# The last head's output weights: one half on partitions 0 to 63 alone, loaded by eight transfers of eight rows

## The chip, the cores and the metric

The kernel runs on one core of a Trainium2 chip. The metric is the device time of one execution in microseconds (us), the median over several runs. All numbers of the profile come from one further execution that the hardware profiler recorded.

## What is computed

One token (a row of 448 numbers) goes through a decode step. The reference, cut to what matters:

```python
xn = layernorm(x)
q  = (xn @ wq) -> 16 heads of 256;  k, v = k_cache, v_cache        # 8 kv heads, 65536 positions, 256 wide
p  = softmax(q . k / 16);  o = p @ v                               # two q heads share one kv head
attn = o.reshape(1, 4096) @ wo                                     # wo is 4096 x 448
moe  = xn + sigmoid(xn @ w_r) * ((silu(xn @ w_gate) * (xn @ w_up)) @ w_down)
out  = x + attn + moe                                              # 448 numbers, bf16
```

The two caches hold 2 x 268 MB, and every byte of them is read once. The output projection `wo` has 256 rows for each of the 16 q heads. This study is about the rows of the last two q heads, 14 and 15, which belong to the last kv head.

## The kernel before, in words

**Stages.** The cache is cut into 32 units (4 for each kv head) of 128 partitions x 128 positions x 256, 8 MB each, which pass through three slots of a ring in SBUF (`ring`, `slots`, line 94). While the K units of one head are transposed and multiplied, the V units of the head before are used. After the last K unit come four V units of the last head (`pe_E`, line 633). The very last V unit is loaded in pieces of 64, 32, 16, 8 and 8 positions (`LAST`, line 15), so that TensorE has little left to do when the last bytes are there.

**Order of the work.** It is written out by hand. `O` records an instruction for an engine, `W` a wait, `item` (line 242) one or several transfers with a semaphore. Every large load is issued by SyncE (SP) in the order in which `item` is called, on one queue, and each waits only for its buffer to come free. A transfer's rows are spread over 16 DMA engines; each of them works through its own share of the queue in order, and the semaphore rises by 1 as each has done its part (by 16 in all).

**The end.** In the order of SP's queue, behind the last pieces of V, stand four loads of `wo` into `kt_all`, a buffer that the K stage no longer needs:

- `wx` (line 312): the rows of kv head 6, 3584 bytes for each of 128 partitions;
- `we0` (`ENDS`, lines 313 to 315): head 14, 1792 bytes for each of 128 partitions (rows 2p and 2p+1 of the head go to partition p);
- `we1` and `we2`: head 15, its even rows and its odd rows, 896 bytes for each of 128 partitions each time.

`ps_s` holds the 448 outputs in four groups of 112 columns on four partitions, so each step of the projection is four matmuls of 112 columns, one for each group (`fin`, `part`, lines 833 to 838). At the end TensorE does this, in order:

- the last 8 positions of V directly, 16 matmuls that add to the transposed result in `ps_m` (`pv_direct`, line 607), while VectorE copies the rest of the result out of `ps_o` (`dve_ob`, line 660);
- 4 matmuls that add this copy, transposed, to the same columns of `ps_m` (`pe_oT`, line 665); VectorE scales them into `oT_sb` (line 686). Column f of head i there holds elements 2p+f of the head on partition p;
- `FIN_X` (line 900): 16 matmuls with `wx`;
- `FIN` 0, 1, 2 (line 909): 8, 4 and 4 matmuls with what `we0`, `we1` and `we2` brought, each group waiting for its load.

Then VectorE and ScalarE copy the sums to SBUF (lines 922 and 923), SP and ScalarE each send one half of the output row, and SP waits for it.

Of the kernel before, what the change touches and what calls it, by code (L numbers as in the profile page):

```python
# [4 lines left out]
BF16 = mybir.dt.bfloat16  # L5
FP32 = mybir.dt.float32
ACTF = mybir.ActivationFunctionType
ALU = mybir.AluOpType
# [4 lines left out]
CH = 64  # L13
# [8 lines left out]
def bass_parallel_sum__gqa_block_cached__moe_arch_mod__decode_kernel(  # L22
# [20 lines left out]
    P = 128  # L43
    _, Hkv, Sk, Dh = A_k_cache.shape
    D = A_x.shape[-1]
    HqDh = A_wq.shape[1]
    Hq = HqDh // Dh
    rep = Hq // Hkv
    F = B_w_gate.shape[1]
    NH = Dh // P  # L50
# [13 lines left out]
    NT = U * (Hkv - 1)  # L64
# [9 lines left out]
    OROWS = 32 * (NG - 1) + 2 * rep  # L74
# [11 lines left out]
    def S_(name, shape, dtype):  # L86
        t = nc.sbuf_tensor(name, shape, dtype)
        sb.append(t)
        return t.__enter__()
# [4 lines left out]
    slots = [ring[:, i * SLOT:(i + 1) * SLOT] for i in range(NSLOT)]  # L94
# [6 lines left out]
    wo_end = kt_all[:, 0:WON]  # L101
    temp = [WQN]

    def T_(n, dtype=BF16):
        n2 = n if dtype == BF16 else 2 * n
        a = slots[2][0:1, temp[0]:temp[0] + n2]
        temp[0] += n2
        assert temp[0] <= SLOT - P
        return a if dtype == BF16 else a.bitcast(dtype)
# [3 lines left out]
    p_sb = S_("p_sb", [P, HC, CH, rep], BF16)  # L113
# [2 lines left out]
    ones_f = S_("ones_f", [P, P], FP32)  # L116
    sel_bf = S_("sel_bf", [P, NG, rep], BF16)
    sel2_bf = S_("sel2_bf", [P, 2, rep], BF16)
    zero_bf = S_("zero_bf", [P, 2 * rep], BF16)
    x_row = T_(D)  # L120
    wr_row = T_(D)
    xe_row = T_(2 * NE * P).rearrange("o (t r p) -> o t r p", t=2, r=NE)
# [22 lines left out]
    hT_sb = S_("hT_sb", [P, 2 * FH], BF16)  # L145
    ob_sb = S_("ob_sb", [P, 2 * Dh], BF16)
    oT_sb = S_("oT_sb", [P, NH, rep], BF16)
    x_f, xc_f, xn_f = T_(D, FP32), T_(D, FP32), T_(D, FP32)
    xn_bf = T_(D)
    stat = S_("stat", [1, 16], FP32)  # L150
# [20 lines left out]
    ps_m = PS_("ps_m", [P, 512], FP32)  # L171
    C_XNT, C_BC, C_TOT, C_OT, C_Q, C_BIG = 0, 16, 18, 22, 28, 64
    C_HT = C_Q
    assert C_Q + NH * Hq + 4 <= C_BIG and C_HT + FK <= C_BIG and C_BIG + P <= 512

    sems = {}
# [33 lines left out]
    def W(e, *key):  # L210
        put(e, "w", key, None, None)
# [3 lines left out]
    def O(e, key, fn, sem=None, n=1):  # L215
        key = key if isinstance(key, tuple) else (key,)
        if not ghost[0]:
            weight[key] = n
        put(e, "o", key, fn, sem or e)
# [22 lines left out]
    def item(key, parts, need=()):  # L242
        for n in need:
            W("sp", *n)
        for ap, src, sem in parts:
            semtot[sem] = semtot.get(sem, 0) + 16
            items[key] = (sem, semtot[sem])
            prog["sp"].append(("d", here[0], ("DMA", key, len(prog["sp"])), (ap, src), sem))
# [16 lines left out]
    def flat_src(src, n):  # L265
        return src.rearrange("a b -> (a b)").rearrange("(p n) -> p n", p=P)

    def wo_src():
        return A_wo[(Hq - rep) * Dh:Hq * Dh, :].rearrange("(i p f) n -> p i f n", i=rep, f=NH)

    def wo_view(t):
        return t.rearrange("p (i f n) -> p i f n", i=rep, f=NH)

    def wo_rows(h0, h1):

# [34 lines left out]
        slot_item("v", t, 0, list(zip(LAST_SEMS, LAST)) if t == NU - 1 else [("slot0", CH), ("half0", CH)],  # L310
                  {c: [("PVC", t - 1, c)] for c in range(HC)})
    item("wx", [(wo_x, wo_rows(HL, HL + 1)[:, 0, :, :].rearrange("p f n -> p (f n)"), "wx")], [("HT",)])
    ENDS = [(0, 0, NH), (1, 0, 1), (1, 1, NH)]
    for k, (i, f0, f1) in enumerate(ENDS):
        item(("wo_end", k), [(wo_view(wo_end)[:, i, f0:f1, :], wo_src()[:, i, f0:f1, :], "we%d" % k)])
    for g, e in enumerate(("sp", "act")):
        late.append((e, g))
    items["out"] = ("out", 16 * len(late))
# [1 line left out]
    def W_item(e, key):  # L320
        W(e, "DMA", key)
# [102 lines left out]
    def mm(*a, **k):  # L424
        return pe.matmul(*a, **k)  # L425
# [181 lines left out]
    def pv_direct(slot, c, lo, hi):  # L607
        def f(it):
            kv = slots[slot].rearrange("p (j d) -> p j d", d=Dh)
            for j in range(lo, hi):  # L610
                for hf in range(NH):
                    ins = mm(ps_m[0:P, C_OT + hf * rep:C_OT + (hf + 1) * rep],
                             lhsT=kv[:, j, :].rearrange("p (d f) -> p d f", f=NH)[:, :, hf], rhs=p_sb[:, c, j - c * CH, :],
                             start=False, stop=False, skip_group_check=True)
            return ins
        return f

# [47 lines left out]
    def pe_oT(t):  # L665
        W("pe", "OB", t)
        W("pe", "RS", min(t, NT))

        def f(it):
            for hf in range(NH):  # L670
                c = C_OT + hf * rep
                for n2 in range(2):
                    lhsT = ob_sb[0:OROWS, n2 * Dh:(n2 + 1) * Dh].rearrange("r (p f) -> r p f", f=NH)[:, :, hf]
                    ins = mm(ps_m[0:P, c:c + rep], lhsT=lhsT, rhs=sel2_bf[0:OROWS, n2, :],
                             start=(n2 == 0 and t < NT), stop=(n2 == 1), skip_group_check=(t >= NT))
            return ins

        O("pe", ("OT", t), f)
        W("dve", "OT", t)
        W("dve", "RS", min(t, NT))  # L680
        src = ps_m[0:P, C_OT:C_OT + NH * rep].rearrange("p (f i) -> p f i", f=NH)
        if t < NT:
            O("dve", ("OTSB", t), lambda it: nc.vector.tensor_tensor(
                out=oT_all[:, :, bass.ds(it[0] * U + it[1], 1), :].rearrange("p f o i -> p f (o i)"), in0=src, in1=rs[:, :, :], op=ALU.mult))
        else:
            O("dve", ("OTSB", t), lambda it: nc.vector.tensor_tensor(out=oT_sb[:, :, :], in0=src, in1=rs[:, :, :], op=ALU.mult))

    def pick(nj):
        return s2[0][:, 0:nj * P] if nj > rep else s2[1][:, 2 * P:2 * P + nj * P]
# [143 lines left out]
    def part(rows, k, g):  # L833
        o = k * D + COLS[g] * DQ
        return rows[:, o:o + DQ]

    def fin(g):
        return ps_s[32 * g:32 * g + 1, 0:DQ]
# [30 lines left out]
    def sums(T):  # L869
        pe_attn2()  # L870
        W_item("dve", "wd")
        O("dve", "XN_AGAIN", lambda it: nc.vector.tensor_scalar(out=xn_again, in0=x_again, scalar1=stat[0:1, 7:8], scalar2=stat[0:1, 4:5],
                                                                op0=ALU.add, op1=ALU.mult))
        W("dve", "XN_AGAIN")
        W("dve", "FFN2")
        W("dve", "ATTN")
        W("dve", "SIG")
        O("dve", "YS", lambda it: nc.vector.scalar_tensor_tensor(  # L878
            out=sum_f, in0=ps_y, scalar=stat[0:1, 6:7], in1=xn_again, op0=ALU.mult, op1=ALU.add))
        W("dve", "YS")  # L880
        O("dve", "YX", lambda it: nc.vector.tensor_tensor(out=sum_f, in0=sum_f, in1=x_again, op=ALU.add))
        W("dve", "YX")
        O("dve", "SUM", lambda it: nc.vector.tensor_tensor(out=sum_f, in0=ps_a, in1=sum_f, op=ALU.add))
        W("pe", "SUM")
        W("pe", "SCOPY", T)

        def fin_base(it):
            for g in range(NF):
                ins = mm(fin(g), lhsT=ones_f[0:1, 0:1], rhs=part(sum_f, 0, g), start=True, stop=False,
                         tile_position=(0, 32 * g), skip_group_check=True)  # L890
            return ins

        O("pe", "FIN_BASE", fin_base)
        O("pe", "OT_ZERO", lambda it: mm(ps_m[0:P, C_OT:C_OT + NH * rep], lhsT=s2[0][:, 0:P], rhs=zero_bf[:, 0:NH * rep], start=True, stop=True,
                                         skip_group_check=True))

    def finish(T):
        W_item("pe", "wx")

        def fin_x(it):  # L900
            for f in range(FO):
                for g in range(NF):
                    ins = mm(fin(g), lhsT=oT_h[:, HL * FO + f:HL * FO + f + 1], rhs=part(wo_x, f, g), start=False, stop=False,
                             tile_position=(0, 32 * g), skip_group_check=True)
            return ins

        O("pe", "FIN_X", fin_x)
        W("pe", "OTSB", T)
        for k, (i, f0, f1) in enumerate(ENDS):
            W_item("pe", ("wo_end", k))  # L910

            def f(it, k=k, i=i, f0=f0, f1=f1):
                for hf in range(f0, f1):
                    for g in range(NF):
                        ins = mm(fin(g), lhsT=oT_sb[:, hf, i:i + 1], rhs=part(wo_end, i * NH + hf, g), start=False,
                                 stop=(k == len(ENDS) - 1), tile_position=(0, 32 * g), skip_group_check=True)
                return ins

            O("pe", ("FIN", k), f)
        W("dve", "FIN", len(ENDS) - 1)  # L920
        W("act", "FIN", len(ENDS) - 1)
        O("dve", "RESULT", lambda it: nc.vector.tensor_copy(out=res_bf[:, DQ:2 * DQ], in_=ps_s[64:97, 0:DQ]), "res")
        O("act", "RESULT2", lambda it: nc.scalar.activation(out=res_bf[:, 0:DQ], in_=ps_s[0:33, 0:DQ], func=ACTF.Copy), "res")
        alias("dve", "RES", sem="res")
        for e, g in late:
            W(e, "RES")
            prog[e].append(("d", here[0], ("OUT", g), (out[0][:, 2 * g * DQ:2 * (g + 1) * DQ], res_bf[32 * g:32 * g + 1, :]), "out"))
# [296 lines left out]
```

## Time and profile before

| | |
|---|---|
| time before, median of 3 runs | 1275.82 us (1275.75 to 1275.88) |
| the profiled execution's own time | 1275.79 us |
| its span, from the first to the last instruction | 1274.5 us |
| busy: TensorE matmul (PE) | 952.0 us (75%) |
| busy: VectorE (DVE), ScalarE (ACT) | 575.6 us (45%), 436.8 us (34%) |
| busy: SP's DMA queue (q1) | 99.8% of 16 engines' span |
| moved | 549.16 MB, mean 431 GB/s |
| granted TensorE clock, mean | 0.894 |

The views of the profile name each operation by its line in the kernel, its engine, its tiles (out<-in) and its shape; nearly all matmuls stand under line 425, the helper that records them, so they are told apart by tiles. PEld is TensorE's loading of weights, which runs beside its matmuls. A view over a stretch of time gives for DMA the share of 16 engines that were busy and the GB/s that they moved.

### The profile page before, as it was taken

What the parts mean: (1) busy time and instruction counts of PE and PEld (TensorE: products, weight loads), DVE (VectorE), ACT (ScalarE), POOL (GpSimd) and SP (SyncE); (2) the same over time, 40 slices, a digit from 0 to 9 for tenths busy, and PEclk for the clock granted to TensorE, in tenths of its full rate; (3) what the DMA queues carried; (4) which work ended last, traced back from release to release, by engine and by line L of the source; (5) the groups of instructions that cost most, each with busy time, mean ns of one, the idle gap of its engine ahead of it and who ended that gap; (6) DMA issues with size and microseconds to landing.
All of it is one profiled execution on the core that took longest, in us unless ns stands there. A gap on an engine that the chain in (4) does not pass through costs nothing.

```text
span 1274.5 us, 23415 instructions
## 1 busy us (share of the span) xinstructions
PE 952.0 (75%) x9665; PEld 620.3 (49%) x9665; DVE 575.6 (45%) x1088; ACT 436.8 (34%) x656; POOL 8.1 (1%) x38
## 2 busy tenths in 40 slices
PE   4998977778777679777778776787777687777754
PEld 2676654445544455444455444454444454444421
DVE  5665644345444455343454444453444544434410
ACT  2454533244332434223333243343333334323300
POOL 2000000000000000000000000000000000000000
PEclk9999998899888899888898888898888998878876
DMA  9999999999999999999999999999999999999998
GB/s 408 428 433 440 436 430 430 436 428 444 432 432 428 436 428 446 432 430 430 434 432 442 432 430 432 432 438 438 430 430 432 432 442 434 430 430 436 418 431 373
DMA packets 12643, 549.16 MB, mean 431 GB/s; under 512 B 1367, under 2 KB 1754, under 8 KB 2906
## 3 DMA queue, kind: packets, MB, share of 16 engines
q1 hardware_dynamic: 12628, 549.03, 99.8%
q8 instruction: 6, 0.10, 0.0%
q14 instruction: 3, 0.02, 0.0%
q10 hardware_dynamic: 6, 0.00, 0.0%
HBM read 549.03 MB, written 0.00 MB: 431 GB/s over the span
## 4 chain that ended last, share of the span: by engine, by line
DMA 77%; PE 19%; ACT 2%; issue 1%; DVE 1%; SPq 0%; ACTq 0%; DVEq 0%
DMA ring<-in_A_v_cache_dram 71%; PE ps_o L425 13%; DMA ring<-in_A_k_cache_dram 5%; PE ps_t L425 3%; PE ps_q L425 2%; ACT kt_all L489 2%; DMA kt_all<-in_A_wo_dram 1%; PE ps_m L425 1%; DVE kt_all L487 0%; ACT S_sb L570 0%; SPq L973 0%; PE ps_s L425 0%; DVE m1p L540 0%; DVE S_sb L538 0%; DVE ring L878 0%
## 5 line engine op out<-in xcount | busy, mean ns | idle before, releaser
L425 PE MATMUL ps_t<-ident_f,ring 128*128 128x128 f32 x4096 | 585.7, 285 | 83.0 <-DMA ring<-in_A_k_cache_dram 59.6
L487 DVE COPY kt_all<-ps_t 128x1024 bf16<-128x1024 bf16 x768 | 487.0, 685 | 290.9 <-PE ps_q L425 286.7
L425 PEld LDWEIGHTS ps_t<-ident_f,ring 128*128 128x128 f32 x4096 | 449.6, 143 | 234.9 <-issue 135.3
L489 ACT ACTIVATE kt_all<-ps_t 128x1024 bf16<-128x1024 bf16 x256 | 262.2, 1024 | 501.0 <-PE ps_q L425 501.0
L425 PE MATMUL ps_o<-ring,p_sb 128*4 128x512 bf16 x2044 | 178.8, 511 | 211.2 <-DMA ring<-in_A_v_cache_dram 206.8
L425 PEld LDWEIGHTS ps_o<-ring,p_sb 128*4 128x4 bf16 x2044 | 53.4, 102 | 301.2 <-issue 277.1
L425 PE MATMUL ps_q<-kt_all,q_cur 128*2 128x512 bf16 x2056 | 164.1, 396 | 0.4 <-DVE kt_all L487 0.3
L511 ACT ACTIVATE s<-ps_q 98x512 bf16<-98x512 f32 x257 | 151.8, 591 | 1.3 <-PE ps_q L425 1.3
L593 DVE RECIPROCAL rs<-ps_m 128x4 f32<-128x4 f32 x29 | 5.3, 183 | 273.8 <-PE ps_m L425 273.8
L580 ACT ACTIVATE p_sb<-S_sb 128x128 bf16<-128x128 bf16 x64 | 18.9, 307 | 273.2 <-PE ps_o L425 273.0
L425 PEld LDWEIGHTS ps_s<-sel_bf,s 128*128 128x128 bf16 x1032 | 64.1, 97 | 5.1 <-ACT s L511 1.9
L425 PE MATMUL ps_s<-sel_bf,s 128*128 128x8 bf16 x1032 | 63.3, 167 | 1.3 <-ACT s L511 1.3
L663 DVE CAST ob_sb<-ps_o 100x512 bf16<-100x512 f32 x29 | 20.1, 692 | 88.8 <-PE ps_o L425 88.8
L425 PEld LDWEIGHTS ps_q<-kt_all,q_cur 128*2 128x2 bf16 x2056 | 26.4, 79 | 45.0 <-issue 45.0
L425 PEld LDWEIGHTS ps_m<-rowsum,ones_f 128*128 128x128 f32 x58 | 12.1, 261 | 21.3 <-issue 21.3
L489 ACT ACT_TABLE_LOAD x7 | 9.0, 1283 | 26.0 <-PE ps_q L425 26.0
L540 DVE TENSOR_REDUCE m1p<-S_sb (+1 forms) x33 | 13.9, 422 | 4.4
L425 PE MATMUL ps_m<-rowsum,ones_f 128*128 128x4 f32 x58 | 14.6, 323 | 0.0
L538 DVE CAST S_sb<-ps_s 128x256 f32 (+1 forms) x33 | 13.7, 415 | 1.9 <-PE ps_s L425 1.9
L570 ACT ACTIVATE S_sb<-S_sb,negmax 128x512 bf16<-128x512 bf16 x16 | 13.2, 852 | 3.2 <-DVE negmax L564 3.2
L425 PE MATMUL ps_m<-diag,ones_f 2*128 2x2 f32 x58 | 11.2, 260 | 3.8 <-DVE diag L555 0.8
L425 PEld LDWEIGHTS ps_m<-diag,ones_f 2*128 2x128 f32 x58 | 8.7, 187 | 10.6 <-DVE diag L555 10.6
(98 smaller groups left out, 126.9 us busy)
## 6 DMA issues: line engine op xcount, KB each, us to landing
ring<-in_A_k_cache_dram SPq DMA_DIRECT2D x10, 4096.0 KB, 28.6
ring<-in_A_v_cache_dram SPq DMA_DIRECT2D x5, 4096.0 KB, 15.7
ring<-in_A_wq_dram SPq DMA_DIRECT2D x1, 2688.0 KB, 11.1
ring<-in_A_wo_dram SPq DMA_DIRECT2D x1, 2688.0 KB, 29.0
ring<-in_A_v_cache_dram SPq DMA_DIRECT2D x1, 2048.0 KB, 10.8
ring<-in_B_w_gate_dram SPq DMA_DIRECT2D x1, 1568.0 KB, 16.7
ring<-in_B_w_up_dram SPq DMA_DIRECT2D x1, 1568.0 KB, 20.0
ring<-in_B_w_down_dram SPq DMA_DIRECT2D x1, 1568.0 KB
```

The lines of the kernel that those rows point to most:

```text
L425: return pe.matmul(*a, **k)
L487: O(e, ("EV", s, m), lambda it: nc.vector.tensor_copy(out=kt[:, :], in_=tb[:, :]), f"ev{m}")
L489: O(e, ("EV", s, m), lambda it: nc.scalar.activation(out=kt[:, :], in_=tb[:, :], func=ACTF.Copy), f"ev{m}")
L511: O("act", ("EVQ", s), lambda it: nc.scalar.activation(out=s2[s % 2][0:QROWS, :], in_=ps_q[0:QROWS, :], func=ACTF.Copy), "evq")
L538: O("dve", ("SCOPY", u), lambda it: nc.vector.tensor_copy(out=S_sb[:, at(it, SBN), :], in_=ps_sn), "sc")
L540: O("dve", ("SMAX", u), lambda it: nc.vector.tensor_reduce(out=m1p[:, :, at(it, 1)], in_=S_sb[:, at(it, SBN), :].rearrange("p n i -> p i n ...
L570: O("act", ("EXP", h, i), lambda it, i=i: nc.scalar.activation(out=S_sb[:, :, i], in_=S_sb[:, :, i], func=ACTF.Exp, bias=negmax[:, i:i + 1 ...
L580: O("act", ("PC", t, c), lambda it: nc.scalar.activation(out=p_sb[:, c, :, :], in_=S_sb[:, n:n + CH, :], func=ACTF.Copy), "pc")
L593: O("dve", ("RS", t), lambda it: nc.vector.reciprocal(out=rs[:, :, :], in_=ps_m[0:P, C_TOT:C_TOT + NH * rep]))
L663: O("dve", ("OB", t), lambda it: nc.vector.tensor_copy(out=ob_sb[0:OROWS, :], in_=ps_o[0:OROWS, :]))
```

## The change

Head 14 keeps its layout and its one transfer. Head 15 is cut in another way: not into even and odd rows, but into rows 0 to 127 (the low half) and rows 128 to 255 (the high half).

- The low half goes to partitions 0 to 63 only, rows 2p and 2p+1 on partition p, 1792 bytes for each. It is loaded by eight transfers that share one semaphore (`we0`); transfer j brings partitions j, j+8, ... j+56. They now stand first, behind `wx`.
- Head 14's transfer comes second (`we1`).
- The high half comes last (`we2`): one row of 896 bytes on each of 128 partitions, into a part of the ring that is free by then (`wo_high`).

For the high half the result is needed in another layout (element 128+p on partition p), for head 15 alone. It goes into one more column of `ps_m` (`C_OTX`), with 8 more matmuls in `pv_direct`, 2 more in `pe_oT`, and one more VectorE operation that scales it into `oT_x`. `FIN` 0 is now 8 matmuls with 64 partitions, `FIN` 1 is 8 with head 14, `FIN` 2 is 4 with the high half and waits for `oT_x` too. The diff without declarations:

```diff
-    ENDS = [(0, 0, NH), (1, 0, 1), (1, 1, NH)]
-    for k, (i, f0, f1) in enumerate(ENDS):
-        item(("wo_end", k), [(wo_view(wo_end)[:, i, f0:f1, :], wo_src()[:, i, f0:f1, :], "we%d" % k)])
+    PL = P // NH
+    low = wo_src(Hq - 1)[0:P, :].rearrange("(p f) n -> p (f n)", f=NH)
+    ENDS = [[(wo_end[j:PL:8, NH * D:2 * NH * D], low[j:PL:8, :]) for j in range(8)],
+            [(wo_end[:, 0:NH * D], wo_src(Hq - 2).rearrange("(p f) n -> p (f n)", f=NH))],
+            [(wo_high, wo_src(Hq - 1)[P:2 * P, :])]]
+    for k, parts in enumerate(ENDS):
+        item(("wo_end", k), [(to, src, "we%d" % k) for to, src in parts])
...
+                ins = mm(ps_m[0:P, C_OTX:C_OTX + 1], lhsT=kv[:, j, P:2 * P], rhs=p_sb[:, c, j - c * CH, rep - 1:rep],
+                         start=False, stop=False, skip_group_check=True)
...
+            for n2 in range(2 if t >= NT else 0):
+                ins = mm(ps_m[0:P, C_OTX:C_OTX + 1], lhsT=ob_sb[0:OROWS, n2 * Dh + P:n2 * Dh + 2 * P],
+                         rhs=sel2_bf[0:OROWS, n2, rep - 1:rep], start=False, stop=(n2 == 1), skip_group_check=True)
...
+            O("dve", ("OTX", t), lambda it: nc.vector.tensor_tensor(
+                out=oT_x[:, 0:1], in0=ps_m[0:P, C_OTX:C_OTX + 1], in1=rs[:, 0, rep - 1:rep], op=ALU.mult))
...
-        for k, (i, f0, f1) in enumerate(ENDS):
+        cols = [[(oT_sb[0:PL, hf, 1:2], wo_end[0:PL, :], NH + hf) for hf in range(NH)],
+                [(oT_sb[:, hf, 0:1], wo_end, hf) for hf in range(NH)],
+                [(oT_x[:, 0:1], wo_high, 0)]]
+        for k in range(len(ENDS)):
             W_item("pe", ("wo_end", k))
+            if k == len(ENDS) - 1:
+                W("pe", "OTX", T)
```

The matmul that clears these columns (`OT_ZERO`, line 894) writes 5 columns instead of 4.

More of the change, by code (lines that the diff above doesn't have):

```diff
@@ L118, in bass_parallel_sum__gqa_block_cached__moe_arch_mod__decode_kernel @@
     sel2_bf = S_("sel2_bf", [P, 2, rep], BF16)
-    zero_bf = S_("zero_bf", [P, 2 * rep], BF16)
+    zero_bf = S_("zero_bf", [P, 3 * rep], BF16)
     x_row = T_(D)
@@ L147, in bass_parallel_sum__gqa_block_cached__moe_arch_mod__decode_kernel @@
     oT_sb = S_("oT_sb", [P, NH, rep], BF16)
+    oT_x = S_("oT_x", [P, 2], BF16)
+    wo_high = slots[1][:, 0:D]
     x_f, xc_f, xn_f = T_(D, FP32), T_(D, FP32), T_(D, FP32)
@@ L173, in bass_parallel_sum__gqa_block_cached__moe_arch_mod__decode_kernel @@
     C_HT = C_Q
+    C_OTX = C_OT + NH * rep
+    assert C_OTX < C_Q and Dh == 2 * P
     assert C_Q + NH * Hq + 4 <= C_BIG and C_HT + FK <= C_BIG and C_BIG + P <= 512
@@ L266, in flat_src, with wo_src @@
         return src.rearrange("a b -> (a b)").rearrange("(p n) -> p n", p=P)
[L268 to L272, printed above, removed]
+    def wo_src(h):
+        return A_wo[h * Dh:(h + 1) * Dh, :]
     def wo_rows(h0, h1):
@@ L893, in sums @@
         O("pe", "FIN_BASE", fin_base)
-        O("pe", "OT_ZERO", lambda it: mm(ps_m[0:P, C_OT:C_OT + NH * rep], lhsT=s2[0][:, 0:P], rhs=zero_bf[:, 0:NH * rep], start=True, stop=True,
+        O("pe", "OT_ZERO", lambda it: mm(ps_m[0:P, C_OT:C_OTX + 1], lhsT=s2[0][:, 0:P], rhs=zero_bf[:, 0:NH * rep + 1], start=True, stop=True,
                                          skip_group_check=True))
@@ L908, in finish, with f @@
         W("pe", "OTSB", T)
-        for k, (i, f0, f1) in enumerate(ENDS):
+        cols = [[(oT_sb[0:PL, hf, 1:2], wo_end[0:PL, :], NH + hf) for hf in range(NH)],
+                [(oT_sb[:, hf, 0:1], wo_end, hf) for hf in range(NH)],
+                [(oT_x[:, 0:1], wo_high, 0)]]
+        for k in range(len(ENDS)):
             W_item("pe", ("wo_end", k))
-            def f(it, k=k, i=i, f0=f0, f1=f1):
-                for hf in range(f0, f1):
+            if k == len(ENDS) - 1:
+                W("pe", "OTX", T)
+            def f(it, k=k):
+                for w, rows, x in cols[k]:
                     for g in range(NF):
-                        ins = mm(fin(g), lhsT=oT_sb[:, hf, i:i + 1], rhs=part(wo_end, i * NH + hf, g), start=False,
+                        ins = mm(fin(g), lhsT=w, rhs=part(rows, x, g), start=False,
                                  stop=(k == len(ENDS) - 1), tile_position=(0, 32 * g), skip_group_check=True)
```

## The prediction

> **What bounds the kernel now.** The page comes first: it says which resource is full.
>
> ```profile
> span 1274.5 us, 23415 instructions
> ...
> q1 hardware_dynamic: 12628, 549.03, 99.8%
> q8 instruction: 6, 0.10, 0.0%
> ```
>
> SP's queue keeps the 16 DMA engines busy for 99.8% of the span, and the change moves the same bytes. So nothing before the last transfers can get shorter; what can move is the way in which the last bytes arrive and what follows them. The chain that ended last, from 1268 us on, shows that end:
>
> ```profile
> 1256.16 15.19 DMA kt_all<-in_A_wo_dram
> 1271.35 0.04 issue
> 1271.40 0.54 PE ps_s L425 x15
> 1271.94 0.13 issue
> 1272.07 0.78 PE ps_s L425 x14
> 1272.85 0.02 issue
> 1272.87 0.28 DVE kt_all L922
> ```
>
> The output weights land at 1271.35 and later, TensorE multiplies, VectorE copies. The timeline of the same microseconds, once as a whole and twice for shorter stretches, shows what each group of matmuls waits for (the bracket is the idle time before it):
>
> ```profile
> 1270.73 0.18 PEld L425 LDWEIGHTS ps_m<-sel_bf,ob_sb 100*128 100x128 bf16 x4
> ...
> 1271.04 0.16 DVE L686 TENSOR_TENSOR oT_sb<-ps_m,rs 128x4 bf16<-128x4 f32 x1 [0.47 <-PE ps_m L425]
> ...
> 1271.40 0.28 PEld L425 LDWEIGHTS ps_s<-kt_all,oT_h 128*1 128x1 bf16 x16 [0.48 <-DMA kt_all<-in_A_wo_dram]
> ...
> 1273.18 0.26 SPq L973 DMA_DIRECT2D out_dram<-kt_all  x1
> ```
> ```profile
> 1272.04 0.13 PEld L425 LDWEIGHTS ps_s<-kt_all,oT_sb 128*1 128x1 bf16 x8 [0.36 <-issue]
> ```
> ```profile
> 1272.29 0.09 PEld L425 LDWEIGHTS ps_s<-kt_all,oT_sb 128*1 128x1 bf16 x4
> 1272.56 0.09 PEld L425 LDWEIGHTS ps_s<-kt_all,oT_sb 128*1 128x1 bf16 x4 [0.17 <-DMA kt_all<-in_A_wo_dram]
> ```
>
> `FIN_X` starts at 1271.40, `FIN` 0 at 1272.04, `FIN` 1 at 1272.29, `FIN` 2 at 1272.56. Sixteen weight loads of `FIN_X` take 0.28 us, so TensorE alone would begin `FIN` 0 at about 1271.7; each group stands where its load landed. From 1272.56 on the rest is fixed: 0.3 us until the copy at 1272.87, and 1.6 us from there to the end at 1274.5. **The end follows the last landing, one to one.**
>
> When do the 16 engines come to the end of the queue? A view by stages of the same execution (its last two columns are the share of the 16 engines and GB/s; a share a little over 1 means that packets overlap):
>
> ```profile
> 1269.00:1269.60 0.60, 0.37 (x4) 0.09 (x4) 0.00 (x0) 0.00 (x0) 0.00 (x0) 0.50 1.01 395
> 1270.10:1270.30 0.20, 0.00 (x0) 0.00 (x0) 0.20 (x1) 0.00 (x0) 0.00 (x0) 0.50 0.93 345
> 1271.00:1271.20 0.20, 0.00 (x1) 0.00 (x0) 0.16 (x1) 0.00 (x0) 0.00 (x0) 0.50 0.55 206
> 1271.30:1271.70 0.40, 0.30 (x16) 0.28 (x16) 0.00 (x0) 0.00 (x0) 0.00 (x0) 0.50 0.41 141
> 1272.10:1272.50 0.40, 0.40 (x12) 0.16 (x12) 0.00 (x0) 0.00 (x0) 0.00 (x0) 0.50 0.00 0
> ```
>
> At 1269 all 16 engines work, 395/16 = 24.7 GB/s each. At 1271.1 it is 206 GB/s, which is eight engines; at 1271.5 it is 141, which is six; by 1272.1 none. So the engines finish over some 2 us, about eight of them before 1271 and eight after. The work was cut into equal shares, so some engines run behind. Views of the DMA at three places tell since when (each transfer ends with one packet of under 512 B on each of its engines):
>
> ```profile
> DMA packets 32, 0.52 MB, mean 477 GB/s; under 512 B 16, under 2 KB 16, under 8 KB 16
> ```
> ```profile
> DMA packets 28, 0.52 MB, mean 477 GB/s; under 512 B 12, under 2 KB 12, under 8 KB 12
> ```
> ```profile
> q8 instruction: 4, 0.07, 0.9%
> ```
>
> The first is from 20.5 to 21.6 us: all 16 engines end one transfer within 1.1 us. The second is from 59.3 to 60.4 us: only 12 do, four lag. The third is from 24 to 52 us, between them: four instruction packets of 16 KB went through the engines, and two more do from 1202 to 1213 us, as the page's six leave and this row says:
>
> ```profile
> q8 instruction: 2, 0.03, 1.2%
> ```
>
> Six instruction packets and six engines that finish last: code loading puts one engine behind each time, and a queue that never runs dry never lets it catch up.
>
> **The change part by part.** What counts is which engines carry the eight small transfers. One row tells how a transfer of few rows is spread, from 1202.7 to 1204.8 us, where 128 rows of `w_down` end and the single row of x follows them on the queue:
>
> ```profile
> DMA packets 146, 0.88 MB, mean 417 GB/s; under 512 B 17, under 2 KB 18, under 8 KB 146
> ```
>
> 17 closing packets: 16 for `w_down`, one for the single row. A one-row transfer runs on one engine, so I take it that eight rows run on eight engines, one row each, and always on the same eight, those that serve partitions 0 to 63 in a full transfer (the *lower* engines). Then a lower engine carries 8 x 1792 B more and 8 x 896 B less than before, an upper one only the 8 x 896 B less.
>
> - *The last landing, if the last engines are upper ones.* Their order becomes `wx`, head 14, high half: the old `we1` load is gone. Eight rows of 896 B cost the last engine 1272.56 - 1272.29 = 0.27 us, the distance of `FIN` 1 and `FIN` 2 (by the rate: 7168 B / 24.7 GB/s = 0.29). **-0.27 us.** The lower engines, +0.3 us, stay behind them, if they belong to those that finished by 1271.
> - *`FIN` 2 waits for two semaphores* instead of one. The only group before that does so is `FIN` 0, for which the gap is 0.13 us of issue, against 0.04 at `FIN_X`: between 0 and 0.09; I take 0.03, since the added wait is over long before. **+0.03 us.**
> - *More matmuls in front of `FIN_X`.* 8 in `pv_direct` and 2 in `pe_oT` at 0.18/4 = 0.045 us are 0.45 at most; in `FIN` 0 and 1 4 more at 0.13/8 = 0.016. What hides them: the 0.48 us in which PEld idles before `FIN_X`. Without that cover `FIN_X` would start up to 0.45 later, at 1271.85, and its 16 loads and those of `FIN` 0 and 1 (0.28 + 0.26) end at 1272.39, so that `FIN` 2 would lose 0.1 of its gain. **0.**
> - *VectorE's added operation* is one more of 0.16 us behind `oT_sb`, done some 0.6 us later than that was (two operations and the later matmuls), near 1271.8, before `FIN` 2 asks for it. **0.**
> - *SP issues 11 transfers where it issued 4.* SP's row:
>
> ```profile
> 1256.16 1.85 SPq L973 DMA_DIRECT2D kt_all<-in_A_wo_dram  x4
> ```
>
>   0.46 us each, so 7 more end at 1261.2 instead of 1258.0. A transfer with few rows may cost less (0.26 for one half of the output, above). The engines come to this place of the queue some 15.19 us after 1256.16, and the earliest of them 2 us before that. Only the output is queued on SP behind, at 1273.18. **0.**
>
> Sum: -0.24 us against this execution, 1275.79 us, which lies 0.03 below the median of the runs: **1275.55 us**.
>
> **The rivals.**
>
> *Last engines among the lower ones (slower).* If one of the six late engines serves partitions 0 to 63, the change adds to the longest queue: eight rows of 1792 B more, which took 1272.04 - 1271.40 = 0.64 us from `FIN_X` to `FIN` 0 (with the 0.13 of issue in it; by the rate 0.58), less the 0.27. That is +0.29 to +0.37 and seven more closing packets: +0.35, **1276.1 us**. It decides as soon as one lower engine lies within 0.6 us of the last. For it: six engines placed by chance would hardly all be upper ones. Against it: the engines come in two groups, eight before and eight after 1271, as two halves of the partitions would; and the one engine that can be named is an early one. From 1202.7 to 1202.8 us, the first 0.1 us of the stretch above:
>
> ```profile
> DMA packets 11, 0.05 MB, mean 520 GB/s; under 512 B 2, under 2 KB 3, under 8 KB 11
> ```
>
> The only packet between 512 B and 2 KB is the row of x, for partition 0, here with the first closing packet of the 17: its engine is the first of all. [...]
>
> *The eight transfers don't pick engines.* If an eight-row transfer is spread over all 16 or over changing engines, each carries the same bytes as before: the last landing stays where it was, within 0.05 us, **1275.8 us**. Against it stands the one closing packet of the one-row transfer. [...]
>
> *Code loads fall elsewhere.* The program grows by some 14 matmuls, 7 transfers and one VectorE operation at its end. If that makes one more 16 KB packet necessary and it meets a late engine, this engine falls back by 16 KB / 24.7 GB/s = 0.66 to 1.7 us (the lag that the late group has), less 0.27: **1276.2 to 1277.2 us**. [...] Against it: the loops, where most of the time goes, keep their code, and ten of 16 engines aren't late.
>
> **How the numbers follow.** Last engines are upper ones: 50%, 1275.4 to 1275.7. A late lower engine: 33%, 1275.9 to 1276.25. No choice of engines, or a gain eaten by the matmuls in front: 12%, 1275.7 to 1275.9. Code loads or something not seen: 5%. The predicted time is the first case's, 1275.55. The range, 1275.35 to 1276.3, takes in the first three cases and the 0.07 us by which runs differ from their median. The bound of 0.2% is 2.55 us, about what a measurement of this kernel can tell from no change; none of the first three cases reaches it, so: faster 1%, same 96%, slower 3%.
>
> **What would show it.** In the stages above the share at 1271.0 to 1271.2 should be about as high as now, the lower engines having taken over what the upper ones lost, and that at 1271.3 to 1271.7 lower. `FIN` 2 should start near 1272.3, `FIN_X` still at 1271.4. If `FIN` 2 starts at 1272.9, late engines are lower ones; if it stays at 1272.56, the transfers don't steer. If `FIN_X` itself moves by more than 0.1 us, either the matmuls in front lost their cover or the engines' lags have changed, by code loads. A change before 1268 us would refute the claim that the rest is untouched.

## The result, and the profile after

The changed kernel takes 1277.53 us (median of 22 runs, 1277.10 to 1278.84) where the kernel before takes 1275.80 (22 runs, 1275.61 to 1276.32): +1.73 us, a ratio of 1.0014 with an interval of 1.0008 to 1.0021. That is slower, by less than the 0.2% of the bound, and outside the stated range of 1275.35 to 1276.3.

The page of the profile after, its span and queue lines:

```profile
span 1276.5 us, 23452 instructions
...
q1 hardware_dynamic: 12612, 549.03, 99.6%
q8 instruction: 6, 0.10, 0.0%
```

The same bytes, and 2.0 us more span. This execution is the longest of the 22 (1278.84 us); their median span is 1276.0, where that of the kernel before is 1274.6 (33 executions timed beside the first four runs below). So the spans differ by 1.4 us by the medians, and some 0.3 of the +1.73 lie outside the span; more on that behind the experiments. The page counts six instruction packets within the span, as before. The stages of the prediction, in the changed kernel (share of 16 engines and GB/s at the end), with one stage more:

```profile
1269.00:1269.60 0.60, 0.34 (x8) 0.08 (x4) 0.00 (x0) 0.00 (x0) 0.00 (x0) 0.50 1.07 390
1270.10:1270.30 0.20, 0.02 (x4) 0.00 (x0) 0.13 (x1) 0.00 (x0) 0.00 (x0) 0.50 0.95 247
1271.00:1271.20 0.20, 0.00 (x0) 0.00 (x0) 0.00 (x0) 0.00 (x0) 0.00 (x0) 0.50 0.53 179
1271.30:1271.70 0.40, 0.40 (x15) 0.40 (x16) 0.00 (x0) 0.00 (x0) 0.00 (x0) 0.50 0.57 190
1272.10:1272.50 0.40, 0.28 (x14) 0.20 (x15) 0.21 (x2) 0.00 (x0) 0.00 (x0) 0.50 0.21 70
1272.60:1273.20 0.60, 0.30 (x16) 0.04 (x4) 0.00 (x0) 0.00 (x0) 0.00 (x0) 0.50 0.07 24
```

Until about 1269.5 all is as before. At 1270.2 the engines are just as busy as before (0.95 against 0.93) but move 247 GB/s, not 345: the packets take longer. The DMA records have them one by one: the packets of `wx` (3584 B) that start from 1269.5 to 1271.0 took 0.141 us each before (median of 54) and take 0.204 now (median of 43). What is lost there is made up late, and in the last stage one engine still works (24 GB/s), where before there was none after 1272.1. The timeline of the end:

```profile
1271.29 0.71 PEld L430 LDWEIGHTS ps_m<-p_sb,ring 128*128 128x128 bf16 x24 [1.68 <-DMA ring<-in_A_v_cache_dram]
...
1272.36 0.28 PEld L430 LDWEIGHTS ps_s<-kt_all,oT_h 128*1 128x1 bf16 x16 [0.20 <-DMA kt_all<-in_A_wo_dram]
...
1274.08 0.13 PEld L430 LDWEIGHTS ps_s<-kt_all,oT_sb 64*1 64x1 bf16 x8 [1.44 <-issue]
...
1274.39 0.10 PEld L430 LDWEIGHTS ps_s<-kt_all,oT_sb 128*1 128x1 bf16 x8 [0.18 <-DMA kt_all<-in_A_wo_dram]
1274.45 0.14 PEld L430 LDWEIGHTS ps_s<-ring,oT_x 128*1 128x1 bf16 x4
```

Two things are new. The last pieces of V and `wx`, which the change doesn't touch, land 1.0 us later: the matmuls of `pv_direct` start at 1271.29, `FIN_X` at 1272.36 instead of 1271.40. In the kernel before, `pv_direct` stood here:

```profile
1270.30 0.51 PEld L425 LDWEIGHTS ps_m<-p_sb,ring 128*128 128x128 bf16 x16 [0.98 <-DMA ring<-in_A_v_cache_dram]
```

And from `FIN_X` to `FIN` 0, the group of the eight small transfers, it is 1.72 us, not 0.64. `FIN` 1 and 2 follow closely. So the end again hangs on the landings, but it is now those of the small transfers that hold it: the last of them is at 1273.98.

### The profile page after: what moved, and what is told of

It reads as the page before. It is cut to its first block, busy times and chain, and to the rows that moved or that the text cites. A ratio compares the mean times of both kernels' runs of the same rounds, so it can differ in the third digit from the quotient of the medians.

```text
span 1276.5 us, 23452 instructions
## 1 busy us (share of the span) xinstructions
PE 955.2 (75%) x9679; PEld 620.3 (49%) x9679; DVE 577.8 (45%) x1089; ACT 436.4 (34%) x656; POOL 11.6 (1%) x38
## 4 chain that ended last, share of the span: by engine, by line
DMA 76%; PE 19%; ACT 2%; issue 1%; DVE 1%; SPq 1%; ACTq 0%; DVEq 0%
DMA ring<-in_A_v_cache_dram 71%; PE ps_o L430 13%; DMA ring<-in_A_k_cache_dram 4%; PE ps_t L430 3%; ACT kt_all L494 2%; PE ps_q L430 2%; PE ps_m L430 1%; DMA kt_all<-in_A_wo_dram 1%; SPq L990 1%; DVE kt_all L492 0%; ACT S_sb L575 0%; PE ps_s L430 0%; DVE m1p L545 0%; DVE S_sb L543 0%; DVE ring L890 0%
## 5 line engine op out<-in xcount | busy, mean ns | idle before, releaser
L430 PE MATMUL ps_o<-ring,p_sb 128*4 128x512 bf16 x2044 | 184.5, 524 | 211.3 <-DMA ring<-in_A_v_cache_dram 206.9
```

## The experiments

Each run was timed beside the kernel before on the same chip; the column on the right is the difference of the two medians. Three theories stood at the start. **P** (partitions): an engine that writes partitions which another engine writes in full transfers gets in its way. **C** (closings): each transfer closes with one packet on each of its engines, and closings of one engine land 0.2 us apart (in the changed kernel the last six from 1273.38 to 1274.38), while its data run ahead. **L**: a late engine is among the lower ones, and nothing else.

| run | engines steered to | rows on foreign partitions (by the assumption in e1) | closings per engine and group | time, us | difference, us |
|---|---|---|---|---|---|
| the change | lower eight | yes | 8 | 1277.53 | +1.73 |
| e1_own | lower eight | no | 8 | 1277.04 | +1.15 |
| e2_one64 | none | yes | 1 | 1276.62 | +0.73 |
| e3_onerow | lower eight | yes | 1 | 1277.04 | +1.15 |
| e4_block | lower eight | yes | 8 | 1277.58 | +1.69 |
| e5_labels (one execution) | none | - | - | 1277.06 | +1.08 |
| e6_onerow_own | lower eight | no | 1 | 1276.13 | +0.15 |
| e7_four | lower eight | no | 4 | 1276.15 | +0.17 |
| e8_halves | none | yes | 2 | 1276.72 | +0.74 |
| e9_eight_small | lower eight, few bytes | no | 8 | 1277.38 | +1.46 |
| e10_one_small | lower eight, few bytes | no | 1 | 1276.13 | +0.21 |
| e11_four_rows | engines 0 to 3 | no | 2 on engines 0 to 3, else 1 | 1276.06 | +0.14 |
| e12_full | none | no | 1 | 1275.98 | +0.08 |

The medians carry the comparison; the intervals of the ratios are about 0.0009 (1.1 us) to each side, so few rows are settled by their intervals alone. What settles it is that rows with one property group together, that the eleven times of e9 (1276.56 to 1277.49) and of e10 (1275.86 to 1276.43) do not overlap, and that the traces show where.

**e1_own: other rows in each transfer.**

```diff
-    ENDS = [[(wo_end[j:PL:8, ...], low[j:PL:8, :]) for j in range(8)],
+    own = [(j // 4 * 32 + j % 4, j // 4 * 32 + 32) for j in range(8)]
+    ENDS = [[(wo_end[a:b:4, ...], low[a:b:4, :]) for a, b in own],
```

> The changed kernel, with other rows in each of the eight transfers: transfer j brings partitions j, j+4, ... j+28 for j below 4, and the same of partitions 32 to 63 for the others. Rows, bytes, packets and completions of every engine stay the same; only which engine writes which partition changes. Theory P (partitions): in the changed kernel an engine writes partitions that another engine writes in all full transfers, and two engines meet at one place of SBUF; now each of the eight engines writes what it always writes, so the slow 1.5 us (229 to 246 GB/s from 1269.5 to 1271.0 at a full share) go away: about 1276.0 us, 1275.5 to 1276.3. Theory C (completions): eight transfers close eight times on each of eight engines, at 0.2 us each (the last landings of the changed kernel are 0.2 us apart): no change, 1277.3 to 1277.7 us. Theory L (a late lower engine and nothing else) gives 1277.5 as well, since the engines' loads are the same.

Measured 1277.04: neither theory's number alone. The trace splits it. Three of its stages, the first of them the time of the slow stretch in the changed kernel:

```profile
1269.50:1271.00 1.50, 1.03 (x29) 0.69 (x26) 0.69 (x1) 0.00 (x0) 0.00 (x0) 0.50 0.91 341
```
```profile
1272.00:1272.40 0.40, 0.00 (x0) 0.00 (x0) 0.00 (x0) 0.00 (x0) 0.00 (x0) 0.50 0.05 18
1272.50:1273.10 0.60, 0.00 (x0) 0.00 (x0) 0.00 (x0) 0.00 (x0) 0.00 (x0) 0.50 0.00 0
```

341 GB/s where the changed kernel has the first of these rows, and the kernel before the second:

```profile
1269.50:1271.00 1.50, 0.60 (x4) 0.09 (x4) 0.69 (x1) 0.00 (x0) 0.00 (x0) 0.50 0.95 238
```
```profile
1269.50:1271.00 1.50, 1.02 (x24) 0.61 (x20) 0.69 (x1) 0.00 (x0) 0.00 (x0) 0.50 0.81 301
```

The kernel before moves fewer GB/s than e1 only because fewer engines still have work (a share of 0.81). What compares is GB/s divided by the share: 375 in e1, 372 before, 251 in the changed kernel. So the slow stretch is gone, as P says, with nothing changed but which engine carries which rows, and so which partitions it writes (e6 against e3 below has the same source rows on every engine). If row i of each transfer goes to the same engine, this edit gives each of the eight engines four neighbouring partitions of 0 to 31 and four of 32 to 63, where the change gave it eight neighbouring ones. That the former are those which the engine writes in a full transfer was my assumption: the DMA records name no partition, and what stands for it is that the slow stretch is gone here and in e6 and e7 (333 and 334 GB/s at 0.86 and 0.87). And no packet moves after 1272.5, yet `FIN` 0 waits until 1273.15:

```profile
1271.42 0.28 PEld L431 LDWEIGHTS ps_s<-kt_all,oT_h 128*1 128x1 bf16 x16 [0.23 <-DMA kt_all<-in_A_wo_dram]
...
1273.15 0.13 PEld L431 LDWEIGHTS ps_s<-kt_all,oT_sb 64*1 64x1 bf16 x8 [1.46 <-issue]
```

In the record of the semaphore the last four increments of `we0` came at 1272.45, 1272.65, 1272.85 and 1273.05, then that of `we1` at 1273.25 and of `we2` at 1273.44: six closings of one engine, 0.2 us apart, after its data had gone through. That is theory C. The last packet of data starts at 1272.35. `wx` landed last at 1271.37, and ten closings of 0.2 us behind it end at 1273.4, so this engine is taken to be one that got `wx` last: a late engine is among the lower eight.

**e2_one64: one transfer of 64 rows.** `ENDS = [[(wo_end[0:PL, ...], low)], ...`

> The changed kernel with one transfer of 64 rows in place of the eight: the same layout and the same matmuls, but all 16 engines carry four rows each and close once. Theory C: the cost was the 64 closings, so it goes: 1275.7 to 1276.0 us. Theory P: 16 engines write to partitions 0 to 63, half of them to partitions that are not theirs, so part of the slow stretch stays: 1276.2 to 1277 us. Theory L: no engine carries more than in the kernel before: 1275.7 to 1275.9 us.

Measured 1276.62, as P has it. Its slow stretch:

```profile
1269.50:1271.00 1.50, 0.69 (x13) 0.26 (x10) 0.69 (x1) 0.00 (x0) 0.00 (x0) 0.50 1.02 262
```

**e3_onerow: one transfer of eight long rows on foreign partitions.** `ENDS = [[(slots[1][0:PL:8, D:D + 8 * NH * D], low8)], ...`

> The changed kernel with the eight transfers replaced by one of eight rows of 14336 B, to partitions 0, 8, ... 56 of the free part of the ring: each of the eight engines carries the same bytes as in the changed kernel, but in one packet, closed once. The computation is changed: FIN 0 multiplies what its buffer held before, not the low half of head 15. Theory C: one closing instead of eight, the 0.2 us steps go: 1275.6 to 1276.2 us, by whether a late engine is a lower one. Theory P: the partitions are still those of other engines, so the slow stretch stays: 1277 us or more. Theory L: 1277.5 us, the same bytes on the same engines.

Measured 1277.04, with 247 GB/s in the slow stretch: P's number, not C's. With one closing only, C cannot be the whole cause.

**e4_block: eight neighbouring partitions in each transfer.** `wo_end[8 * j:8 * j + 8, ...]`

> The changed kernel with eight neighbouring partitions in each of the eight transfers: transfer j brings partitions 8j to 8j+7. Rows, bytes and closings of every engine stay the same, but eight engines now write into eight neighbouring partitions at a time. Theory P: four engines at each place instead of two, worse than the changed kernel: 1278 us or more. Theory C and theory L: no change, 1277.3 to 1277.7 us.

Measured 1277.58, no worse than the change, with 298 GB/s in the stretch: P's number missed, that of C and L held. That more engines at one place cost more is not borne out; the engines run up to 2 us apart (the 16 landings of one transfer lie 1.94 us apart near 1258 in the trace before), so the eight rows of one transfer need not meet, but this was not tried further.

**e5_labels: which engines are late.** The kernel before with `item("mk", [(..., n rows of 20 + n elements) for n in 1..15])` behind the first loads of `wo`.

> The kernel before with 15 tiny transfers behind the first loads of wo, of 1, 2, ... 15 rows with 42 to 70 bytes each, each row length used by one transfer only: if a transfer of n rows runs on the n lowest engines, the number of such packets that an engine carries tells which engine it is. Theory L, in its sharpened form after the first four runs: of the six engines that finish last one carries rows of the lower half, five of the upper half; a lower one among them is what the steered rows must not meet. If all six were upper ones, a late lower engine could not explain the last 1.0 us of the changed kernel. Time as before, within 0.5 us.

The transfer with n rows left exactly n packets in the DMA records, and each step of n brought one engine more. Their lag behind engine 0 near 1210 us, in us:

```
engine   0    1    2    3    4    5    6    7    8    9    10   11   12   13    14
lag     0.00 0.90 0.17 0.99 0.73 1.68 1.50 0.15 0.33 2.33 1.63 1.64 0.02 -0.04 0.14
```

Late are 5, 6, 9, 10 and 11; the record can't name engine 15, and the sixth instruction packet starts at 1210.87, in the midst of this place. Two lower engines are late, so my first case, all late engines upper, does not hold in this execution. The time, 1277.06 in one execution, missed the half microsecond that I gave it: in this execution the engines' landings of one transfer lay 2.5 us apart already near 60 us (1.9 in the kernel before), and `wx` landed 0.6 to 1.6 us later on them. What the 15 small transfers did to that was not followed up.

**e6_onerow_own: the steering alone.** As e3, but `slots[1][0:32:4, ...]`, partitions 0, 4, ... 28.

> The changed kernel with the eight transfers replaced by one of eight rows of 14336 B to partitions 0, 4, ... 28, those that the eight engines write in full transfers too: the same bytes on the same engines, one closing each, no foreign partition. The computation is changed: FIN 0 multiplies what its buffer held before, not the low half of head 15. Theories P and C together: both costs are gone, only the steering is left: with one late lower engine 1276.1 us (1275.9 to 1276.3), as my prediction's first rival had it; without one 1275.55. If neither P nor C holds and the layout with 64 partitions and more matmuls costs by itself: 1276.6 us as with one transfer of 64 rows, or more.

Measured 1276.13, +0.15, against e3 with the same packets and +1.15: only the partitions differ. The slow stretch is gone:

```profile
1269.50:1271.00 1.50, 1.04 (x23) 0.53 (x24) 0.69 (x1) 0.00 (x0) 0.00 (x0) 0.50 0.86 333
```

**e7_four: four closings.** Four transfers of eight rows of 3584 B, `slots[1][j:32:4, ...]`.

> The same with four transfers of eight rows of 3584 B, partitions j, j+4, ... j+28 for transfer j: the same bytes on the same engines, four closings each, no foreign partition. The computation is changed as in the run with one transfer of eight rows. Theory C: a closing takes 0.2 us, so four take 0.8 us, about 0.2 more than the bytes (0.58): 0.2 us above the run with one closing, 0.7 below the one with eight (1277.04): 1276.3 us. If the time of a packet and not the closing counts: the same time as with one closing.

Measured 1276.15, as with one closing. Theory C in the form that I wrote down (0.2 us above e6) is not seen. That the closings do take their 0.2 us is in the trace: the last four of `we0` land at 1271.63, 1271.85, 1272.06 and 1272.27, with 0.14 us of data for each. Those of `we1` and `we2` follow at 1272.55 and 1272.83, the last 1.39 us behind the landing of `wx`, where the data of the three loads take 1.45 by the rate (0.58, 0.58, 0.29). So C has to be put otherwise: a backlog of closings costs only what the bytes behind it don't cover. Four closings take 0.8 us beside 0.58 us of data, and the two loads behind them bring 0.9 us of data with only two closings. This account was made after the result.

**e8_halves: foreign partitions in the kernel before.** Head 14's load in two transfers of 64 rows: `halves = ((0, P // 2), (P // 2, P))` for the first of `ENDS`.

> The kernel before with head 14's load cut into two transfers of 64 rows each, partitions 0 to 63 and 64 to 127: the same layout, the same matmuls, the same bytes on every engine, two closings instead of one. Theory P by itself: 64 rows on 16 engines give an engine partitions that another one writes in full transfers, so a stretch with full share and few GB/s appears, as with one transfer of 64 rows: 1276.4 to 1277 us. Theory C: one closing more, hidden behind the bytes: 1275.9 us. If the source rows or the other buffer made the slow stretch: 1275.9 us too.

Measured 1276.72, +0.74. Nothing but the cut of one transfer was changed, and the slow stretch is there:

```profile
1269.50:1271.00 1.50, 0.68 (x7) 0.17 (x7) 0.69 (x1) 0.00 (x0) 0.00 (x0) 0.50 1.01 273
```

**e9_eight_small and e10_one_small: closings in the kernel before.** `item("mk", ...)` behind `we0`: eight transfers of eight rows of 512 B, or one of eight rows of 4096 B, on the engines' own partitions by the assumption in e1.

> The kernel before with eight transfers of eight rows of 512 B added between head 14's load and the even rows of head 15; they go to a free part of the ring, on the partitions that their engines write in full transfers too, and nothing uses them. The bytes are few (4 KB on each lower engine, 0.17 us at 24.7 GB/s), the matmuls are those of before. Theory C: on a late lower engine eight closings of 0.2 us stand in front of the last two loads, 1.6 us of which the bytes of the queue cover only a part; from the landing of wx at least 11 closings, 2.2 us, where before it was 1.16: about 1.0 us more, 1276.7 to 1277.1 us. If closings are free and the extra of the changed kernel's eight transfers lay in their rows or in the new layout: 1276.0 to 1276.2 us.

> The same with one transfer of eight rows of 4096 B at the same place: the same bytes on the same engines, one closing instead of eight. Both theories: 1276.0 to 1276.2 us, by the 0.17 us of bytes on a late lower engine. Theory C is the difference to the run with eight small transfers, 0.6 us or more; without it the two runs agree.

Measured 1277.38 and 1276.13: the same bytes, 1.25 us apart. The first lies above the 1277.1 that theory C gave. Three of its eleven executions took only 1276.6, which was not followed up. The group behind the small transfers, `FIN` 1, in the run with eight (where `FIN` 2 follows in the same row) and in the run with one:

```profile
1273.87 0.29 PEld L428 LDWEIGHTS ps_s<-kt_all,oT_sb 128*1 128x1 bf16 x8 [1.62 <-DMA kt_all<-in_A_wo_dram]
```
```profile
1272.66 0.09 PEld L427 LDWEIGHTS ps_s<-kt_all,oT_sb 128*1 128x1 bf16 x4 [0.28 <-DMA kt_all<-in_A_wo_dram]
```

In the run with eight, the last packet of data starts at 1272.31, and the increments go on until 1274.03. At the end two engines step side by side, 0.2 us each (1273.39 and 1273.43, 1273.59 and 1273.63), so the distance belongs to the engine and not to the semaphore. Head 14's load landed last at 1272.02; ten closings of 0.2 us from there give 1274.02. The last landing is 2.57 us behind that of `wx`, where it is 1.16 in the kernel before: +1.41, near the measured +1.46. The expectation counted too little, because it left out the time that head 14's data take before the first closing.

**e11_four_rows: the steering with early engines.** Half of the low half in one transfer of four rows (`slots[1][0:16:4, ...]`), the rest in 128 pieces of 448 B.

> The changed kernel with rows 0 to 63 of head 15 in one transfer of four rows of 14336 B (partitions 0, 4, 8, 12, so engines 0 to 3, which the run with the labels showed 0 to 1 us behind the first, none of them late) and rows 64 to 127 in one transfer of 128 pieces of 448 B over all 16 engines. The computation is changed: FIN 0 multiplies what its buffer holds, not the low half of head 15 in its place. This is the steering of the change with the right engines, one closing and no foreign partition. If the prediction's first case is right as a mechanism, the late engines carry 8 x 448 B less than before, 0.15 us, while engines 0 to 3 carry 0.43 us more and are still in time: 1275.75 us, 0.1 to 0.2 us under the kernel before in the same runs. If a transfer of few rows costs something else, it isn't faster than before.

Measured 1276.06, +0.14; not faster, so the number missed; the median span, though, is 1274.5 against 1274.6 in the kernel before, and six of the eleven times lie more than 1.4 us above their span (see below). In its trace the last landing comes 1.01 us after that of `wx` (1272.61 and 1271.60), before it was 1.16 (1272.51 and 1271.35): the 0.15 is there. But `wx` itself landed 0.25 later than before, and the last pieces of V too, by 0.2, ahead of everything that this run changes.

**e12_full: the rest of the change.** The low half in one transfer of 128 rows of 896 B.

> The changed kernel with the low half loaded by one transfer of 128 rows of 896 B to all partitions: every engine carries the bytes that it carried before, with as many closings as before, and writes only its own partitions; what is left of the change are its 14 more matmuls, the VectorE operation more, the other order of the loads and the other buffer. The computation is changed: FIN 0 multiplies what its buffer holds on partitions 0 to 63, not the low half in its place. If these parts are hidden, as the prediction has it: the time before, within 0.2 us (builds of this kernel start that much apart), 1275.8 to 1276.1 us. If the added matmuls or the layout cost by themselves: 1276.4 us or more, and then part of what theories P and C take is theirs.

Measured 1275.98, +0.08. The added matmuls, the VectorE operation, the order and the other buffer cost nothing that shows in the span (median 1274.6, as before). Three of the eleven executions took 1276.9 to 1277.1 with the same span.

**The time outside the span.** In 102 executions of the kernel before, timed beside these runs, the time is 1.3 or 1.4 us longer than the span. In the changed kernel it is 1.5 us or more longer in 12 of 22, up to 2.3. The traces show what has become different there: a seventh instruction packet. It stands in eight of the nine traces of the changed kernel and of the runs built on it (not in e11, where the time is 1.5 us above the span), and in none of the five traces of the kernel before and of the runs built on that. In the changed kernel it starts at 1277.76, 1.25 us behind the last instruction, where the page no longer counts it (a view from 1276.5 to 1279 us):

```profile
q8 instruction: 1, 0.02, 3.3%
```

In the changed kernel, e2 and e4 it starts 1.25 or 1.26 us behind the last instruction, and these are the profiled executions whose time is 2.0 to 2.3 us above the span; in the five others it starts at most 0.45 us behind the end, and the difference is 1.3. In those three the packet's end, counted from the first instruction, lies 0.23 us above the measured time, each time. That the longer program makes the packet necessary, and that these executions end with it, is argued from this; no run sets it apart.

## Why the prediction was wrong

**The sum of what was measured.** The parts come from differences of runs: the rest of the change +0.08 (e12); steering eight engines +0.07 (e6 less e12); eight closings instead of one +1.00 (e1 less e6); foreign partitions +0.58 (the change less e1). Together +1.73. That they add up exactly is arithmetic, since each is the difference of two neighbours in one chain of runs. The shares depend on the order: with one closing, foreign partitions cost +1.00 (e3 less e6), not +0.58, and from e1 to e6 the size of the packets and the buffer change too. That two of them are causes by themselves is shown by e9 against e10 (+1.25) and by e8 against the kernel before (+0.74). By the median spans the parts are 0.0 for the rest, 0.0 for steering, 1.0 for the closings and 0.4 for foreign partitions; the other 0.3 or so lies outside the span.

**The step that failed** is the price of the eight transfers. The forecast's sum puts it at nothing, and the first rival names "seven more closing packets" but gives with them a sum, +0.35, that lies within what the bytes alone make (+0.29 to +0.37). No case of the prediction reaches 1277.53. A closing packet is short in the DMA record (4 B, 0.009 us), and I took the record for the cost. Its landing at the semaphore is what TensorE waits for (in e1 `FIN` 0 starts at 1273.15, behind a landing at 1273.05, with the last data packet at 1272.35), and the landings of one engine come 0.2 us apart there; eight in place of one cost +1.00 us (e1 less e6). The trace before could not show it, since there each load of the end brought 0.26 us of data or more between two closings of an engine.

**The second failure** is the sentence that eight rows run on those engines "that serve partitions 0 to 63 in a full transfer". That each such transfer runs on the same eight engines was right, as e5's counts show. The partitions were not, if the assumption in e1 holds: by it a lower engine serves four neighbouring partitions of 0 to 31 and four of 32 to 63, and the transfers' rows j, j+8, ... gave most engines rows of others. No trace names the partitions of an engine; that partitions count is shown by e3 against e6, with the same packets (+1.15 and +0.15). So I looked at which engines carry how many bytes, and not at where they write; the forecast's sum has no term for it, and it cost +0.58 us (the change less e1).

**The choice of the likeliest case** was wrong as well: engines 5 and 6 are late in the run that names them, and in e1 one lower engine gets `wx` last. The two groups of eight that I read as halves of the partitions were not there: in the trace before, `we2` lands on six engines by 1270.84, on four from 1271.17 to 1271.70, and on six from 1272.26 to 1272.51. The first rival, a late lower engine, had the case right and its price wrong: in place of +0.35, e6, where both other costs are gone, took +0.15 by its time and nothing by its span. In its trace the late lower engine is not the one that got `wx` last: the last row of `we0` landed at 1271.91, 0.36 us behind the last landing of `wx`, while such a row's data take 0.58.

**What held.** The end follows the last landing, 1.95 to 2.03 us behind it in eleven of the traces and 2.13 in the three others (the change, e1 and e4), where the last groups of matmuls have to be worked off together. The 14 added matmuls and `OTX` are hidden (e12). SP's longer list of issues is hidden too, though my aside that a transfer with few rows may cost less there was wrong:

```profile
L990 SPq DMA_DIRECT2D kt_all<-in_A_wo_dram x10: 430/563/688, 1256.4 to 1261.9; - x10
```

The shortest of the ten took 0.43 us, and the median, which is that of small ones, 0.56; the list ends at 1262.8, not at 1261.2. The rival that the transfers don't pick engines is refuted by e5's counts. The rival that code loads fall elsewhere came true in part. No packet more meets the loads of the end, and nothing moves before 1269; but a seventh instruction packet comes at the end of the program, and by the median some 0.3 us of the +1.73 lie outside the span, where it stands. My signposts named two causes for a later `FIN_X`, cover lost or code loads, and it was a third, the slow stretch.

**What stays open.** Single executions differ by 0.25 us before the end begins (`wx` lands last at 1271.35 in the trace of the kernel before and at 1271.60 in those of e10 and e11), so the +0.07 of steering and whether steering to early engines can win 0.15 us can't be told from this. No version with a faster time than the kernel before came out. Why the packets of a full transfer are slowed too, as those of `wx` are (0.204 us against 0.141), was not tried, and neither was e4's missing extra. What the seventh instruction packet costs was not tried by itself.

## What to carry to other kernels

Where the end of a kernel hangs on the last transfers, count their closings per engine and not only their bytes: eight small transfers in a row landed 0.2 us apart here (e1, e9), and four cost nothing with 0.9 us of data behind them (e7: +0.17, e6 with one: +0.15). Try a transfer of few rows on more than one set of partitions: eight rows on 0, 4, ... 28 cost +0.15 us and the same packets on 0, 8, ... 56 +1.15 (e6 and e3), and with transfers of 64 rows 262 and 273 GB/s moved in the slow stretch at a full share (e2 and e8; 301 at a share of 0.81 before). Before steering work to some engines, name the late ones: 15 transfers of 1 to 15 rows labelled 15 of the 16 in one trace (e5), for that execution. And compare spans as well as times: here a part of the difference lay behind the last instruction.

## What the runs showed of the hardware that was not expected

- One engine's closings land 0.2 us apart while less data than that lies between: 1272.45 to 1273.44 for six of them in e1, with no packet moving any more; the same 0.2 us with 512 B (e9) and 1792 B (e1) for each, 0.21 with 3584 B (e7).
- In the changed kernel the packets of a full transfer were slower too: those of `wx` took 0.204 us, 0.141 before. From 1269.5 to 1271.0 us, GB/s divided by the share of busy engines is 251 to 301 in the five runs with rows on foreign partitions (by the assumption in e1; 238 to 298 GB/s at 0.91 to 1.02), and 363 to 387 in the others (301 to 395 GB/s at 0.81 to 1.02).
- A transfer of n rows, n from 1 to 15, ran on n engines, and each row more added one engine to the same set (e5: n packets for n rows).
- The semaphore of the eight transfers in e1 shows eight single increments from 1257.39 to 1262.06, while SP issued them, and 64 more when the data were there.
- A lag between the engines that is there early is not made up: in the trace before, the 16 landings of one transfer lie 1.03 us apart near 21 us, 1.86 near 60 and 1.94 near 1258, with the queue busy for 99.8% of the span.
